# Attention and MLP block: three PV visits for four per group of MLP slots, and six PSUM banks shared by maxima and exps

## The chip, the cores and the metric

The kernel runs on one core of one Trainium2 chip. The metric is the device time of one execution in microseconds (us). Before the change the median of three runs is 1621.18 us.

## The reference

The input is layer-normalised; attention with 32 heads of 16 columns and an MLP (512 to 1792 to 512, squared ReLU) both read the normalised rows; the output is x plus attention times the SiLU of the MLP. All is fp32, 2048 rows.

```python
scores = jnp.einsum("bhqd,bhkd->bhqk", q, k) * (Dh ** -0.5)
p = _softmax(scores, axis=-1)
o = jnp.einsum("bhqk,bhkd->bhqd", p, v)
...
h = jnp.einsum("bsd,df->bsf", x, w1) + b1
r = jnp.where(h > zero, h, zero)
h = r * r
out = jnp.einsum("bsf,fd->bsd", h, w2) + b2
...
xn = _layernorm(x, axis=-1)
s = _A_ref(xn, A_wqkv, A_wo)
g = _silu(_B_ref(xn, B_w1, B_b1, B_w2, B_b2))
return x + s * g
```

## The kernel before

Work is cut into 32 units (four heads x 512 queries) of 16 key blocks (128 keys) each, so 512 slots. For every unit the kernel makes three things, each in its own stretch of time, one behind the other like a pipeline:

- the **maxima** ("m"): one matmul of queries against 512 keys into a PSUM bank (`max_mm`, matmul on L320), and VectorE's reduction of that bank to one column (L327). 64 per unit, four per slot, 24 slots ahead (LEAD). When a unit's last is made, `max_end` folds its maxima (L335), and six slots later `shift` transposes them (L371) and sends them through DRAM into rows of the unit's exp operands.
- the **exps** ("s"): one matmul of 128 keys against 512 queries of one head (`exp_mm`, L1286), whose operand rows already hold the subtracted maximum, and ScalarE's exp of that bank into SBUF (L1298). Four per slot.
- the **PV visit** (`pv_step`, `pv_mm`, L406): for one key block, four heads side by side in the four 32-column strips of the array, 512 queries each, added up in one bank (`po`) over 16 visits. Each of the four matmuls is two instructions in the trace (x8 per block). One visit stood at the end of every slot, for the block of two slots before.

Maxima and exps have a depth of 64 rows, so two of them run at once on the two row halves of the array; such a half is a "lane". Into the lane that is free goes the MLP: its matmuls are cut into 64-row halves too ("D"). A **round** is one instruction (or one pair of 256 columns) on each lane. Both lanes of a D accumulate into the same bank (`pd_t`), so the second lane may start only when the first is done with it: `block` gives the first D of a lane a wait (`last_use`) on the reader of a maximum or exp that the other lane issued after its last D.

Most MLP slots come in long groups of four (`block` yields 12 D units per lane, `long_slots` places them). First-layer groups (`first_pair`) have two 256-column matmuls per unit, second-layer groups (`second`) one of 512. A group before: ten rounds of lane 0's D with a maximum or exp on lane 1, a visit, two rounds with D and two with maximum and exp on both lanes, a visit; then the same with the lanes exchanged. That is 28 rounds, 16 maxima, 16 exps and four visits. When lane 1's D end, `post` has ScalarE read the bank `pd_t` (for the first layer two ReLUs, L568).

PSUM has eight banks: three in pool `pe` (`se`, for exps), three in pool `pm` (`pm_t`, for maxima), one `pd_t` and one `po`. A bank is used again, in turn within its pool, when its reader is done.

The order of TensorE, ScalarE, VectorE, GpSimd and the DMA queue (SP) is that in which the code issues (manual schedules); nothing is reordered. Slot ends also issue the loads and stores (`begin`, `max_end`, `shift_due`).

Of the kernel before, what the change touches and what calls it, by code (L numbers as in the profile page):

```python
# [9 lines left out]
F32 = mybir.dt.float32  # L10
# [7 lines left out]
P = 128  # L18
# [32 lines left out]
    [(0, 0), (0, 2), (1, 0), (1, 2), (2, 0), (2, 2)],  # L51
    [(0, 1), (0, 3), (1, 1), (1, 3), (2, 1), (2, 3)],
)
EPS = 1e-5


@with_exitstack
def kernel(
# [56 lines left out]
    with ExitStack() as ph:  # L115
# [136 lines left out]
        def block(mms, per, post, between={}):  # L252


            def emit(ms, lane, follow):
                r = slice(64 * lane, 64 * lane + 64)
                for out_, lh, rh, first_, last_ in ms:
                    mm = nc.tensor.matmul(  # L258
                        out_, lh(r), rh(r),
                        start=first_ and lane == 0, stop=last_ and lane == 1,  # L260
                        skip_group_check=True,
                    )
# [24 lines left out]

# [21 lines left out]
        for m4 in m4s:  # L309
            nc.vector.memset(m4, 0.0)  # L310

        def max_mm(j, bank=None):
            u, p, qb, kc = next(stream[j])
            qd = u // 4
# [5 lines left out]
            nc.tensor.matmul(  # L320
                ps,
                qms[u][p][64 * j : 64 * j + 64, qb * P : (qb + 1) * P],
                kas[qd, p][64 * j : 64 * j + 64, kc * 512 : (kc + 1) * 512],
                start=True, stop=True,
            )
            c = (2 * p + j) * 4 + qb
            return nc.vector.tensor_reduce(  # L327
                mxs[u][:, c, kc : kc + 1], ps, axis=AX.X, op=ALU.max
            )
# [948 lines left out]
        def exp_mm(st, j, pts, spare):  # L1278
            u, kb = divmod(st, 16)
            qd = u // 4  # L1280
            b = 64 * (j % 2)
            if spare:
                se = bank() if wos.get("banks") else pm.tile([P, 512], F32, name="pm_t")
            else:
                se = pe.tile([P, 512], F32, name="se")
            nc.tensor.matmul(  # L1286
                se, kas[qd, j // 2][b : b + 64, kb * P : (kb + 1) * P],
                qes[u][j // 2][b : b + 64, :],
                start=True, stop=True,
            )  # L1290
# [7 lines left out]
            return nc.scalar.activation(pts[j], se, AF.Exp, scale=0.25)  # L1298
# [201 lines left out]
        def dense():  # L1500
            mp = ExitStack()
            yield from mlp_tasks(mp)
            mp.close()
            early.close()
            wo_pools()
            wo_load(0, [0, 1, 2])
            wo_ask(0)
            wo_ask(1)
            for _ in range(2):
                yield [], None  # L1510
# [33 lines left out]
        def slot(st, mms, post):  # L1544
# [54 lines left out]
            for i in range(len(other)):  # L1599
                if i < len(own):  # L1600
                    own[i]()
                if spare and lane == 0 and i == len(mms) - 1:

                    use = nc.vector.tensor_scalar(seen, done_d[0][:, :1], 1.0, 0.0, op0=ALU.mult, op1=ALU.add)
                if other[i] is not None:
                    follow = other[i]()
                    if i >= len(own) - 1 and use is None:
                        use = follow
            last_use[0] = None if post is not None or spare and lane else use
            if post is not None:  # L1610
                post()
            max_end(g)

        def long_slots(st0, units, post):


            g0 = st0 + LEAD
# [4 lines left out]
            def s(lane):  # L1622
                kb, j = todo[lane].pop(0)
                return exp_mm(kb, j, pts[kb], False)

            for h in range(2):
                own, other = units[h], 1 - h
                for part, (mine, theirs) in enumerate((("D" * 10, "msmsmsmsms"), ("DDss", "mmsm"))):
                    st = st0 + 2 * h + part
                    if st > st0:  # L1630
                        begin(st)
                    for i, ops in enumerate(zip(mine, theirs)):
                        for lane in (h, other) if part else (other, h):
                            o = ops[0] if lane == h else ops[1]
                            if o == "D":
                                own.pop(0)()
                            elif o == "m":
                                max_mm(lane)
                            else:
                                use = s(lane)  # L1640
                                if part and lane == h and i == 2:
                                    last_use[0] = use
                        if part and h and i == 1 and post is not None:
                            post()
# [5 lines left out]
            assert not todo[0] and not todo[1] and not units[0] and not units[1]  # L1650

        def plain_slot(st):

# [14 lines left out]
        def begin(st):  # L1668
            now[0] = st
            if st % 64 == 48 and st // 64 + 1 < NQ:  # L1670
                load_v(st // 64 + 1)
            run_waiting()

        done = FIRST
        for st_ in range(NU * 16):
            if st_ < done:
                continue
            begin(st_)
            if st_ == FIRST:
                qs.close()  # L1680
            item = next(dn, None)
            if st_ == FIRST:

                for g in (LEAD, LEAD + 1):
                    max_end(g)
                for fn in last_store:
                    fn()
            if item is not None and len(item) > 2:
                assert st_ % 4 == 0
                long_slots(st_, *item[:2])  # L1690
# [9 lines left out]
            pv_step(st_ - 2, pts.pop(st_ - 2))  # L1700
        assert not [1 for it in stream for _ in it] and not left
        run_waiting(True)
        assert not waiting and next(dn, None) is None
# [29 lines left out]
```

## Time and profile before

| | |
|---|---|
| runs (three) | 1620.95 to 1621.23 us, median 1621.18 |
| profiled execution | span 1619.6 us from first to last instruction |
| granted TensorE clock | 1.00 throughout |
| stretch 165 to 1450 us (groups and other MLP slots) | TensorE busy 1285.0, VectorE 1132.1, ScalarE 992.7, GpSimd 380.4 us |
| idle time of VectorE ahead of maxima in that stretch | 151.8 us |

The profile comes from one execution. No time is shown for it but its span; the timed runs are 1.6 us longer than this. A busy share of TensorE says little, because matmuls overlap and their ends are modelled; start times of rounds and visits say more. In the rows, PE is the matmul, PEld the loading of its weights, which waits where a bank is not free. "64*128" and "128*32" name the rows and columns of the array that a matmul uses.

### The profile page before, as it was taken

To read this page: it belongs to the slowest core of one execution; us is meant where nothing else is said; L and a number is where in the kernel's file an instruction comes from. 1 tells how busy PE (TensorE), PEld (TensorE's weight loads), DVE (VectorE), ACT (ScalarE), POOL (GpSimd) and SP (SyncE) were. 2 spreads that over 40 slices of the span, in tenths; PEclk is the share of its full clock that TensorE was granted. 3 is DMA by queue.
4 is the path that set the end of the run, shared out by engine and by line. 5 is a ranking of instruction groups with operands and counts; after the bars stand their busy time and mean duration, and the time that the engine had idled before them with its cause. 6 is when DMAs were issued, how large, how long until landed. Compare 5 with 4: busy or idle time off the path is not lost.

```text
span 1619.6 us, 36065 instructions
## 1 busy us (share of the span) xinstructions
PE 1607.3 (99%) x13660; PEld 939.7 (58%) x13660; DVE 1352.4 (84%) x2307; ACT 1187.2 (73%) x2347; POOL 534.1 (33%) x610
## 2 busy tenths in 40 slices
PE   8999999999999999999999999999999999999998
PEld 7799665556545654664466446645654565445543
DVE  7486888888888888888888888888888888887754
ACT  7212777777777777877777777777777777778886
POOL 6436667133113311331133113311331123214621
PEclk9999999999999999999999999999999999999999
DMA  8967556434333333423333334323432252237655
GB/s 290 244 237 234 174 156 160 132 96 128 81 104 94 106 88 88 131 87 101 90 107 100 91 89 118 115 71 90 131 107 73 65 163 76 64 102 228 207 177 169
DMA packets 164173, 209.19 MB, mean 129 GB/s; under 512 B 59136, under 2 KB 79360, under 8 KB 162432
## 3 DMA queue, kind: packets, MB, share of 16 engines
q1 hardware_dynamic: 163856, 206.63, 43.9%
q8 instruction: 108, 1.77, 0.5%
q14 instruction: 65, 0.53, 0.1%
q10 hardware_dynamic: 144, 0.26, 0.0%
HBM read 148.90 MB, written 56.34 MB: 127 GB/s over the span
## 4 chain that ended last, share of the span: by engine, by line
PE 99%; DVE 1%; DMA 0%; issue 0%; ACT 0%; DVEq 0%
PE po L406 31%; PE pd_t L258 19%; PE pm_t L320 17%; PE se L1286 15%; PE pd_t L226 5%; PE pm_t L1157 4%; PE pm_t L226 1%; PE pd_t L1157 1%; PE se L1127 1%; PE se L1061 1%; PE se L320 1%; PE pm_t L1248 0%; PE pd_t L1127 0%; DVE mx L327 0%; PE po L1061 0%; DMA xt<-in_A_x_dram 0%
## 5 line engine op out<-in xcount | busy, mean ns | idle before, releaser
L327 DVE TENSOR_REDUCE mx<-pm_t 128x1 f32<-128x512 f32 x1910 | 1188.3, 684 | 174.5 <-PE pm_t L320 84.8
L1298 ACT ACTIVATE pt<-se 128x512 f32<-128x512 f32 x1894 | 975.4, 613 | 234.3 <-PE se L1286 187.0
L320 PE MATMUL pm_t<-ka,qm 64*128 64x512 f32 x1910 | 761.0, 419 | 0.0
L1286 PE MATMUL se<-qe,ka 64*128 64x512 f32 x2005 | 677.3, 396 | 0.0
L406 PE MATMUL po<-pt,v 128*32 128x512 f32 x3820 | 520.8, 605 | 0.2 <-DVE tsm L849 0.2
L320 PEld LDWEIGHTS pm_t<-ka,qm 64*128 64x128 f32 x1910 | 335.2, 184 | 236.0 <-DVE mx L327 224.5
L1286 PEld LDWEIGHTS se<-qe,ka 64*128 64x128 f32 x2005 | 338.9, 184 | 19.8 <-ACT xr L1298 1.7
L258 PEld LDWEIGHTS pd_t<-xc,w1s 64*128 64x128 f32 x2352 | 292.1, 187 | 82.2 <-issue 82.2
L258 PE MATMUL pd_t<-xc,w1s 64*128 64x256 f32 x2352 | 332.3, 288 | 0.0
L258 PE MATMUL pd_t<-w2t,hT 64*128 64x512 f32 x1080 | 300.1, 410 | 0.0
L258 PEld LDWEIGHTS pd_t<-w2t,hT 64*128 64x128 f32 x1080 | 179.3, 184 | 82.4 <-issue 75.5
L571 POOL TENSOR_TENSOR r<-r 128x512 f32<-128x512 f32 x56 | 58.2, 1040 | 353.5 <-ACT r L568 353.5
L406 PEld LDWEIGHTS po<-pt,v 128*32 128x32 f32 x3820 | 76.7, 108 | 147.1 <-issue 125.6
L327 DVE TENSOR_REDUCE mx<-se 128x1 f32<-128x512 f32 x121 | 77.9, 686 | 26.1 <-PE pm_t L1157 17.3
L590 POOL TENSOR_TENSOR u<-u,b_t 128x512 f32<-128x512 f32 x16 | 20.6, 1285 | 209.1 <-ACT u L589 209.1
L568 ACT ACTIVATE r<-pd_t,b_t 128x256 f32<-128x256 f32 x112 | 46.9, 470 | 57.1 <-PE pd_t L258 55.0
L99 POOL TENSOR_SCALAR sh<-tr 128x32 fp32r<-128x32 f32 x30 | 6.5, 217 | 213.6 <-DVE tr L371 213.6
L1157 PE MATMUL pm_t<-xT,wr_t 64*128 64x512 f32 x408 | 74.0, 388 | 0.0
L100 POOL TENSOR_TENSOR hT<-r,hT 128x512 fp32r<-128x512 f32 x56 | 72.2, 1290 | 4.7
L226 PE MATMUL pd_t<-w2t,hT 64*128 64x512 f32 x264 | 68.7, 392 | 0.0
L1157 PEld LDWEIGHTS pm_t<-xT,wr_t 64*128 64x128 f32 x408 | 60.7, 185 | 0.0
L455 POOL TENSOR_TENSOR ot<-ot,hl 128x512 f32<-128x512 f32 x27 | 34.7, 1285 | 65.4 <-DMA hl<-r_d 51.7
(177 smaller groups left out, 1398.9 us busy)
## 6 DMA issues: line engine op xcount, KB each, us to landing
w1s<-w_d SPq DMA_DIRECT2D x196, 256.0 KB
qm<-q_d SPq DMA_DIRECT2D x384, 32.0 KB
ka<-k_d SPq DMA_DIRECT2D x96, 128.0 KB
qe<-q_d SPq DMA_DIRECT2D x384, 32.0 KB
q_d<-hl SPq DMA_DIRECT2D x16, 512.0 KB
g<-g_d SPq DMA_DIRECT2D x32, 256.0 KB
k_d<-hl SPq DMA_DIRECT2D x15, 512.0 KB
on_d<-hl SPq DMA_DIRECT2D x116, 64.0 KB
```

Of the source, the lines that this page charges most:

```text
L100: (lo or nc.gpsimd).tensor_tensor(dst[1], raw, dst[0].bitcast(F32), op=ALU.subtract)
L226: mm = nc.tensor.matmul(out_, lh(r), rh(r), start=first_ and lane == 0, stop=last_ and lane == 1, skip_group_check=True,)
L258: mm = nc.tensor.matmul(out_, lh(r), rh(r), start=first_ and lane == 0, stop=last_ and lane == 1, skip_group_check=True,)
L320: nc.tensor.matmul(ps, qms[u][p][64 * j : 64 * j + 64, qb * P : (qb + 1) * P], kas[qd, p][64 * j : 64 * j + 64, kc * 512 : (kc + 1) * 512] ...
L327: return nc.vector.tensor_reduce(mxs[u][:, c, kc : kc + 1], ps, axis=AX.X, op=ALU.max)
L406: nc.tensor.matmul(po[32 * j : 32 * j + 32, :], vs[qd][:, (4 * kb + j) * VW : (4 * kb + j) * VW + 32], pts[j], start=(kb == 0), stop=(kb = ...
L455: nc.gpsimd.tensor_tensor(ot, ot, rb, op=ALU.mult)
L568: nc.scalar.activation(r[:, i], ps[:, i * CW : (i + 1) * CW], AF.Relu, bias=b1_t[:, fo : fo + 1])
L571: nc.gpsimd.tensor_tensor(r, r, r, op=ALU.mult)
L1157: mm = nc.tensor.matmul(out_, lh(r), rh(r), start=first_ and lane == first, stop=last_ and lane != first, skip_group_check=True,)
L1286: nc.tensor.matmul(se, kas[qd, j // 2][b : b + 64, kb * P : (kb + 1) * P], qes[u][j // 2][b : b + 64, :], start=True, stop=True,)
L1298: return nc.scalar.activation(pts[j], se, AF.Exp, scale=0.25)
```

## The change

`long_slots` gets its order from a string of 32 letters per group, m for a maximum and s for an exp, one for the first layer and one for the second. The group still has 28 rounds: 12 with lane 0's D, one with both lanes on maxima or exps, a visit of two key blocks, 12 with lane 1's D, a visit of one, three rounds with both lanes, a visit of one. The lane whose turn it is to start waits for the maximum or exp that the other lane issued in the round with both lanes. Slot ends fall behind rounds 7, 14, 21 and 28.

The six banks of `pe` and `pm` become one set (`spots`). A small account of times (`flow`, with constants for a round, a visit and the readers) is kept while the program is built; each maximum or exp takes the bank that this account expects to be free first. The account fixes which bank is used, and nothing else; at run time a matmul waits for its bank's real reader.

```diff
+DOUBLE = (12, 25, 26, 27)
+VISITS = {13: 2, 25: 1, 28: 1}
+QUARTERS = (7, 14, 21, 28)
+ORDERS = ("msmsmsmsmmsmmsmssmmsssmsmsmsssmm", "msmsmssmsmsmmsmssmmsmmssmssmssmm")
...
-            ], post, 4
+            ], post, ORDERS[per == 1]
...
+        def flow_start():
+            spots.extend([0, pe.tile([P, 512], F32, name="se")] for _ in range(3))
+            spots.extend([0, pm.tile([P, 512], F32, name="pm_t")] for _ in range(3))
+            flow["on"] = True
...
+        def flow_bank(kind):
+            at, t = spots.pop(min(range(len(spots)), key=lambda i: spots[i][0]))
+            flow["pe"] = max(flow["pe"], at)
+            every, held = READERS[kind]
+            begin_ = max(flow[kind], flow["pe"] + READY)
+            flow[kind] = begin_ + every
+            spots.append([begin_ + held, t])
+            return t
...
-            if spare:
+            if flow["on"]:
+                se = flow_bank("s")
+            elif spare:
...
-        def long_slots(st0, units, post):
+        def long_slots(st0, units, post, order):
...
+            ops, st, pv_at, fence = list(order), st0, st0 - 2, None
...
+            for r in range(len(order) - 4):
+                if r in QUARTERS:
+                    st += 1
+                    begin(st)
+                if r in DOUBLE:
+                    uses = [qk(lane) for lane in range(2)]
+                    done_lane = 0 if units[1] else 1
+                    if fence != done_lane:
+                        fence = done_lane
+                        last_use[0] = uses[done_lane]
+                else:
+                    h = 0 if units[0] else 1
+                    qk(1 - h)
+                    units[h].pop(0)()
+                    if not units[1] and post is not None:
+                        post()
+                flow_round()
+                if r + 1 in QUARTERS:
                     max_end(st + LEAD)
                     shift_due(st + 1 + LEAD)
-                    pv_step(st - 2, pts.pop(st - 2))
+                for _ in range(VISITS.get(r + 1, 0)):
+                    pv_step(pv_at, pts.pop(pv_at))
+                    pv_at += 1
+                if r + 1 in VISITS:
+                    flow_visit(VISITS[r + 1])
```

The order of TensorE in a first-layer group, first at the middle of the group. The rows are line, instruction, output and operands with buffer numbers, shape, and what the instruction waits for (DVE is VectorE, Activation ScalarE, DMAHW a load). Before, with D on L258, maxima on L320, exps on L1286 and PV on L406, from the tenth round on:

```order
L1286 MATMUL se_7326<-qe2_738,ka2_734 128x512 [waits Activation_49]
L258 MATMUL pd_t_7279<-xc_6197,w1s3_1510 128x256 x2
L406 MATMUL po_7240<-pt16_1494,v1_1789 32x512
L406 MATMUL po_7240<-pt10_1488,v1_1789 32x512
L406 MATMUL po_7240<-pt0_1478,v1_1789 32x512
L406 MATMUL po_7240<-pt12_1490,v1_1789 32x512
L258 MATMUL pd_t_7279<-xc_6197,w1s3_1510 128x256 x2
L320 MATMUL pm_t_7340<-ka0_207,qm0_204 128x512 [waits DVE_49]
L258 MATMUL pd_t_7279<-xc_6197,w1s3_1510 128x256 x2
L320 MATMUL pm_t_7345<-ka0_207,qm0_204 128x512 [waits DVE_49]
L1286 MATMUL se_7348<-qe2_738,ka2_734 128x512 [waits Activation_49]
```

Of the change (D on L268, maxima on L357, exps on L1325, PV on L443), the round with both lanes, the double visit and lane 1's first D:

```order
L357 MATMUL se_2470<-ka0_207,qm0_204 128x512 [waits DMAHW3_49,DMAHW4_49,DMAHW2_49,Activation_49]
L1325 MATMUL pm_t_2473<-qe3_739,ka3_735 128x512 [waits DVE_49]
L443 MATMUL po_6360<-pt1_1479,v1_1789 32x512
L443 MATMUL po_6360<-pt10_1488,v1_1789 32x512
L443 MATMUL po_6360<-pt0_1478,v1_1789 32x512
L443 MATMUL po_6360<-pt13_1491,v1_1789 32x512
L443 MATMUL po_6360<-pt2_1480,v1_1789 32x512
L443 MATMUL po_6360<-pt11_1489,v1_1789 32x512
L443 MATMUL po_6360<-pt3_1481,v1_1789 32x512
L443 MATMUL po_6360<-pt5_1483,v1_1789 32x512
L357 MATMUL pm_t_2472<-ka0_207,qm0_204 128x512 [waits Activation_49]
L268 MATMUL pd_t_6389<-xc_5531,w1s0_1507 128x256 [waits DVE_49]
```

The visit of one block that cut lane 0's D is gone and eight PV matmuls stand together; the exp ahead of them waits for VectorE, and so does lane 1's first D, for the maximum in the first row.

The second place is that of the banks, from round 6 of the same group on. Before:

```order
L320 MATMUL pm_t_7311<-ka0_207,qm0_204 128x512 [waits DVE_49]
L258 MATMUL pd_t_7279<-xc_6197,w1s2_1509 128x256 x2
L1286 MATMUL se_7316<-qe3_739,ka3_735 128x512 [waits Activation_49]
L258 MATMUL pd_t_7279<-xc_6197,w1s2_1509 128x256 x2
L320 MATMUL pm_t_7321<-ka0_207,qm0_204 128x512 [waits DVE_49]
L258 MATMUL pd_t_7279<-xc_6197,w1s2_1509 128x256 x2
```

Of the change:

```order
L357 MATMUL pm_t_2473<-ka0_207,qm0_204 128x512 [waits DVE_49]
L268 MATMUL pd_t_6389<-xc_5531,w1s2_1509 128x256 x2
L1325 MATMUL se_2470<-qe3_739,ka3_735 128x512 [waits Activation_49]
L268 MATMUL pd_t_6389<-xc_5531,w1s2_1509 128x256 x2
L357 MATMUL pm_t_2471<-ka0_207,qm0_204 128x512 [waits DVE_49]
L268 MATMUL pd_t_6389<-xc_5531,w1s2_1509 128x256 x2
L357 MATMUL se_2469<-ka0_207,qm0_204 128x512 [waits Activation_49]
L268 MATMUL pd_t_6389<-xc_5531,w1s3_1510 128x256 x2
L1325 MATMUL pm_t_2472<-qe2_738,ka2_734 128x512 [waits DVE_49]
```

Maxima now go into `se` banks and exps into `pm_t` banks, and either waits for the other's reader: the first row puts the group's fourth maximum into pm_t_2473, the bank that the exp of round 12 (second row of the piece above) takes next.

More of the change, by code (lines that the diff above doesn't have):

```diff
@@ L53 @@
 )
+DOUBLE = (12, 25, 26, 27)
+VISITS = {13: 2, 25: 1, 28: 1}
+QUARTERS = (7, 14, 21, 28)
+ORDERS = ("msmsmsmsmmsmmsmssmmsssmsmsmsssmm", "msmsmssmsmsmmsmssmmsmmssmssmssmm")
+ROUND = 232
+FIRST_ROUND = 335
+STEP = 907
+VISIT = 185
+READY = 450
+READERS = {"s": (476, 675), "m": (600, 745)}
 EPS = 1e-5
@@ L310, with flow_round, flow_visit @@
             nc.vector.memset(m4, 0.0)
+        flow = {"on": False, "pe": 0, "s": 0, "m": 0, "fresh": False}
+        spots = []
+        def flow_start():
+            spots.extend([0, pe.tile([P, 512], F32, name="se")] for _ in range(3))
+            spots.extend([0, pm.tile([P, 512], F32, name="pm_t")] for _ in range(3))
+            flow["on"] = True
+        def flow_round():
+            flow["pe"] += FIRST_ROUND if flow["fresh"] else ROUND
+            flow["fresh"] = False
+        def flow_visit(n):
+            flow["pe"] += VISIT + n * STEP
+            flow["fresh"] = True
+        def flow_bank(kind):
[6 more added lines that the diff above has]
+            return t
         def max_mm(j, bank=None):
             u, p, qb, kc = next(stream[j])
+            if bank is None and flow["on"]:
+                bank = lambda: flow_bank("m")
             qd = u // 4
@@ L1612, in slot @@
             max_end(g)
[L1614 to L1617 removed]
+        def long_slots(st0, units, post, order):
+            if not spots:
+                flow_start()
             todo = [[(st0 + k, j) for k in range(4) for j in (lane, lane + 2)] for lane in range(2)]
@@ L1620, in long_slots, with qk @@
                 pts.setdefault(kb, {})
-            def s(lane):
+            ops, st, pv_at, fence = list(order), st0, st0 - 2, None
+            def qk(lane):
+                if ops.pop(0) == "m":
+                    return max_mm(lane)
                 kb, j = todo[lane].pop(0)
                 return exp_mm(kb, j, pts[kb], False)
[L1626 to L1644, printed above, removed]
@@ L1645, in long_slots @@
                     max_end(st + LEAD)
                     shift_due(st + 1 + LEAD)
-                    pv_step(st - 2, pts.pop(st - 2))
+                for _ in range(VISITS.get(r + 1, 0)):
[3 more added lines that the diff above has]
+                    flow_visit(VISITS[r + 1])
             if post is not None:
                 last_use[0] = None
-            assert not todo[0] and not todo[1] and not units[0] and not units[1]
+            assert not ops and not todo[0] and not todo[1] and not units[0] and not units[1]
```

5 lines of the change are left out of this document (4 added, 1 removed).

## The prediction, made before the changed kernel ran

> **What bounds the kernel now.** I read the page first, then the chain of waits, then the timeline of single engines inside the MLP stretch.
>
> ```profile
> span 1619.6 us, 36065 instructions
> PE 1607.3 (99%) x13660; PEld 939.7 (58%) x13660; DVE 1352.4 (84%) x2307; ACT 1187.2 (73%) x2347; POOL 534.1 (33%) x610
> PE 99%; DVE 1%; DMA 0%; issue 0%; ACT 0%; DVEq 0%
> ```
>
> The third line is the chain that ended last: TensorE is 99% of it. VectorE is next with 84% busy. The chain in order of time shows the beat of the long groups: L406 x8 is one PV visit, and the second row of each pair is the fourth visit after the first (the three between are left out).
>
> ```profile
> 833.14 0.99 PE po L406 x8
> ...
> 844.55 1.00 PE po L406 x8
> ...
> 1058.79 1.00 PE po L406 x8
> ...
> 1070.12 0.99 PE po L406 x8
> ```
>
> So a group of four slots takes 844.55 - 833.14 = 11.41 us with 256-column MLP work (first layer) and 1070.12 - 1058.79 = 11.33 us with 512 columns (second layer). Their number comes from the MLP matmuls, grouped by form; a group issues 48 of the first kind or 24 of the second:
>
> ```profile
> L258 PE MATMUL pd_t<-xc,w1s 64*128 64x256 f32 x2352 | 332.3, 288 | 0.0
> L258 PE MATMUL pd_t<-w2t,hT 64*128 64x512 f32 x1080 | 300.1, 410 | 0.0
> L258 PE MATMUL pd_t<-ka,w1s 64*128 64x256 f32 x336 | 47.4, 287 | 0.0
> ```
>
> (2352 + 336) / 48 = 56 groups of the first kind, 1080 / 24 = 45 of the second, 101 in all. One microsecond more or less per ten groups is already 10 us. The timeline of TensorE gives the parts of a group; the columns are start, length, and instruction:
>
> ```profile
> 832.76 0.39 PE L1286 MATMUL se<-qe,ka 64*128 64x512 f32 x1
> 833.07 1.06 PE L406 MATMUL po<-pt,v 128*32 128x512 f32 x8
> 834.07 0.50 PE L258 MATMUL pd_t<-xc,w1s 64*128 64x256 f32 x2
> 834.41 0.40 PE L258 MATMUL pd_t<-xc,w1s 64*128 64x256 f32 x2
> 834.65 0.40 PE L258 MATMUL pd_t<-xc,w1s 64*128 64x256 f32 x2
> ...
> 836.33 0.40 PE L258 MATMUL pd_t<-xc,w1s 64*128 64x256 f32 x2
> 836.66 1.07 PE L406 MATMUL po<-pt,v 128*32 128x512 f32 x8
> ...
> 601.11 0.39 PE L258 MATMUL pd_t<-w2t,hT 64*128 64x512 f32 x1
> ...
> 602.98 0.39 PE L258 MATMUL pd_t<-w2t,hT 64*128 64x512 f32 x1
> ```
>
> From a round's start to the visit: 0.31 us (833.07 - 832.76) or 0.33 (836.66 - 836.33). From the visit to the next round: 1.00 (834.07 - 833.07). The first round behind a visit: 0.34 (834.41 - 834.07); any other: 0.24, and in the second layer 1.87 / 8 = 0.234.
>
> **What the change takes away.** The number of rounds stays 28. One visit of four goes and its key block moves into another visit. Only the end of the program shows several key blocks in one visit, three of them:
>
> ```profile
> 1605.41 0.62 PE L406 MATMUL po<-xl,v 128*32 128x512 f32 x1
> ...
> 1606.30 1.90 PE L406 MATMUL po<-xr,v 128*32 128x512 f32 x16
> 1608.13 0.50 PE L895 MATMUL pm_t<-wot,q 64*128 64x512 f32 x1
> ```
>
> Three blocks take 1608.13 - 1605.41 = 2.72, one takes 1.00, so each further one (2.72 - 1.00) / 2 = 0.86; the second alone reads 0.89 (1606.30 - 1605.41). I take 0.86. Per group that saves 1.00 - 0.86 on the block, 0.10 on a first round that becomes an ordinary one, and 0.08 on a last one: 0.32 us, 101 x 0.32 = 32 us at most. The Trainium skill (TensorEngine Tiling (Array Packing), Tiling Modes) says that changing the tiling mode drains the engine; the 1.00 against 0.86 agrees, and by that rule alone the result would be the first rival below, 1589.
>
> **What it adds: waits on VectorE.** The first phase now holds 13 rounds without a visit. In the first layer these issue maxima in rounds 0, 2, 4, 6, 8, 9, 11 and 12 (eight), in the second in 0, 2, 4, 7, 9, 11 and 12 (seven). VectorE's rows:
>
> ```profile
> 832.52 1.89 DVE L327 TENSOR_REDUCE mx<-pm_t 128x1 f32<-128x512 f32 x3 [0.54 <-PE pd_t L258]
> 834.60 3.08 DVE L327 TENSOR_REDUCE mx<-pm_t 128x1 f32<-128x512 f32 x5 [0.19 <-PE pd_t L258]
> 601.30 3.08 DVE L327 TENSOR_REDUCE mx<-pm_t 128x1 f32<-128x512 f32 x5 [0.19 <-PE pm_t L320]
> 602.64 0.18 PEld L320 LDWEIGHTS pm_t<-ka,qm 64*128 64x128 f32 x1 [0.19 <-DVE mx L327]
> 602.73 0.41 PE L320 MATMUL pm_t<-ka,qm 64*128 64x512 f32 x1
> ```
>
> A maximum lasts 0.68 (the first row of the next fence) and one follows the other every (3.08 - 0.68) / 4 = 0.60. The first starts 0.53 behind the round (834.60 - 834.07). A bank is free late: the second of the five from 601.30 ends at 601.30 + 0.60 + 0.68 = 602.58, the weight load that waited for it starts at 602.64, its matmul at 602.73, so 0.06 and 0.09 later.
>
> By the order on record the exp of round 12 goes into the bank of the fourth maximum (0, 2, 4, then 6 or 7). That one starts at 0.53 + 3 x 0.60 = 2.33, ends at 3.01, lets the load go at 3.07 and the matmul at 3.16. Without the wait round 12 starts at 0.34 + 11 x 0.24 = 2.98, or 2.91 in the second layer. So 0.18 or 0.25 us of TensorE time is lost ahead of the double visit, and behind the waiting exp stand the visit and every later round; nothing hides it. The double visit ends at 3.16 + 0.31 + 0.86 + 1.00 = 5.33.
>
> The first D of the other lane waits, in the first layer, for the eighth maximum: 0.53 + 7 x 0.60 + 0.68 + 0.06 = 5.47. Its load may come 0.34 - 0.24 = 0.10 behind the visit's end without loss, at 5.43; so 0.04 more. With seven maxima it is done at 4.87, free.
>
> The phases: A 5.37 (5.33 in the second layer); B, twelve rounds and a visit, 0.34 + 10 x 0.24 + 0.33 + 1.00 = 4.07 (4.01); C, three rounds and a visit, 0.34 + 0.24 + 0.31 + 1.00 = 1.89. Sums 11.33 and 11.23, against 11.41 and 11.33: 56 x 0.08 + 45 x 0.10 = **9.0 us saved** of the 32.
>
> **What else lands in the full phase.** Once per 16 slots VectorE also folds the maxima (L335) and transposes them (L371):
>
> ```profile
> 401.41 0.68 DVE L327 TENSOR_REDUCE mx<-pm_t 128x1 f32<-128x512 f32 x1
> 402.13 0.22 DVE L335 TENSOR_REDUCE m<-mx 128x16 f32<-128x64 f32 x1
> 402.29 1.89 DVE L327 TENSOR_REDUCE mx<-pm_t 128x1 f32<-128x512 f32 x3
> 416.69 0.20 DVE L371 STREAM_TRANSPOSE tr<-m 128x32 f32<-128x32 f32 x1
> ```
>
> The fold stretches 0.60 to 0.88 (402.29 - 401.41). It comes behind C's last maximum, where VectorE has 1.89 + 0.53 - (0.53 + 3 x 0.60) = 0.09 to spare, so 0.19 goes into phase A. The transpose now comes behind round 6, in phase A too: 0.20 less the overlap of 0.08, 0.12. Before, the idle 0.54 and 0.19 in the rows above took both. 28 units x 0.31 = 8.7 us at most, nothing at least; four or five of the transposes meet slots outside the groups, so I take 7.
>
> Edits at nothing: ScalarE,
>
> ```profile
> 832.79 0.84 ACT L568 ACTIVATE r<-pd_t,b_t 128x256 f32<-128x256 f32 x2 [1.03 <-PE pd_t L258]
> 833.52 4.01 ACT L1298 ACTIVATE pt<-se 128x512 f32<-128x512 f32 x8
> L1298 ACT ACTIVATE pt<-se 128x512 f32<-128x512 f32 x1799 | 923.8, 613 | 225.1 <-PE se L1286 180.3 <-PE pd_t L258 39.2 <-PE pm_t L320 4.4
> ```
>
> exps every (4.01 - 0.61) / 7 = 0.49, 16 per group and a pair of 0.84 make 8.7 of 11.3 us; the pair now has a visit, phase C and a visit (3.2 us) before the next group needs its bank, so it is covered; if two exps stood ahead of it, it would still be. PV of a block comes six rounds or more behind its last exp. What SP and POOL issue at slot ends moves by three rounds at most (slot ends at rounds 7, 14, 21, 28 in place of 10, 14, 24, 28), earlier everywhere; if a load were late after all, it would be q or k of the next unit, once per 16 slots. The 44 other MLP slots keep their orders and only get common banks: nothing, by the same 0.60 and 0.49.
>
> **Sum.** The span of 1619.6 lies 1.6 us under the median of 1621.2, which is taken as constant: 1621.2 - 9.0 + 7.0 = **1619 us**.
>
> The Trainium skill speaks against the change on the same page (Performance Considerations, PSUM Bottleneck): tiling speeds up TensorE and not the emptying of PSUM, which can become the bound. The rows agree with 0.60 us per maximum against 0.24 per round; without that page the sum is the same.
>
> **Rivals.** (1) The waits don't bite, because the maxima start earlier than the bank rows say: phase A is 2.98 + 0.31 + 1.86 = 5.15 or 5.08, everything is saved, 1621 - 32 = 1589. For it speaks that VectorE's mean share would be only 84% x 11.4 / 11.1; against it that 13 rounds last 3.3 us and their maxima 4.2 to 4.8. If half of each wait goes, 1604. (2) **Slower:** the second block of a visit costs nearly a whole visit in mid-program, because its operands come fresh from ScalarE there and not at the end: place, the 101 double visits; price up to 1.00 - 0.86 = 0.14 each, 14 us, 1633. It decides from 0.03 on, since only 2 us are left to lose. Then the change does not do what it says either. Against it is the row at 1606.30. (3) The late D restarts the pair. A late load elsewhere did:
>
> ```profile
> 915.20 0.40 PE L320 MATMUL pm_t<-ka,qm 64*128 64x512 f32 x1
> 915.47 0.18 PEld L1286 LDWEIGHTS se<-qe,ka 64*128 64x128 f32 x1 [0.29 <-ACT pt L1298]
> 915.82 0.39 PE L320 MATMUL pm_t<-ka,qm 64*128 64x512 f32 x1
> ```
>
> The round behind it came after 0.35 in place of 0.24. In 56 groups 0.11 is 6 us: 1625 to 1627 with the whole 8.7 above.
>
> **How the numbers follow.** Forecast (saved and lost nearly even, 1610 to 1625) 55%, of which 25 points lie under 1618, 27 within 0.2% and 3 above; rival 1, whole or half, 17%; rival 3, 16%, of which 2 within 0.2%; rival 2, 12%. A measurement of this kernel tells about 0.2%, 3.2 us, from no change. Faster 25 + 17 = 42%, same 27 + 2 = 29%, slower 3 + 14 + 12 = 29%. The range reaches up to rival 2's price, and down to past the half case of rival 1; its full case and the rest, under 2 in 10, stay out: 1599 to 1633.
>
> **What would show it.** In the changed profile: three visits per group, the double one 1.86 from start to next round (1.00 + 1.00 would be rival 2); a group of 11.33 and 11.23, not 11.1 (rival 1); TensorE's weight loads waiting for VectorE some 0.2 us once per group ahead of the double visit; groups with a fold or a transpose longer by 0.1 to 0.2. Wrong would be the whole if TensorE waited elsewhere, for ScalarE or a load, or if VectorE's interval changed with the common banks.

## The result, and the profile after

The changed kernel takes **1630.25 us** (median of four runs, 1630.05 to 1630.42), the kernel before beside it 1621.2 us. The ratio is 1.0055 with a 95% interval of 1.0043 to 1.0067: slower by about 0.55%. The forecast was 1619 us, so a little faster; the time lies inside the range of 1599 to 1633, on the wrong side of 1621.

The lines of the page that answer to those of before (span; busy time by engine; the chain that ended last):

```profile
span 1628.6 us, 37052 instructions
PE 1615.3 (99%) x13660; PEld 973.0 (60%) x13660; DVE 1348.9 (83%) x2307; ACT 1199.9 (74%) x2347; POOL 535.5 (33%) x610
PE 98%; ACT 1%; DVE 1%; issue 0%; DMA 0%; DVEq 0%
```

The span grew by 1628.6 - 1619.6 = 9.0 us, as the timed runs did. TensorE is still the chain. The page doesn't tell more, since TensorE counts as busy while rounds follow each other more slowly. The starts of the PV visits do (timeline of TensorE after the change; start, length, instruction; x8 is one key block, x16 two; L443 is L406 of before):

```profile
379.34 1.07 PE L443 MATMUL po<-pt,v 128*32 128x512 f32 x8
383.83 1.92 PE L443 MATMUL po<-pt,v 128*32 128x512 f32 x16
388.86 1.06 PE L443 MATMUL po<-pt,v 128*32 128x512 f32 x8
390.75 1.07 PE L443 MATMUL po<-pt,v 128*32 128x512 f32 x8
```

The phases, from here on always from visit to visit: A (a visit, 13 rounds) 383.83 - 379.34 = 4.49, B (the double visit, 12 rounds) 5.03, C (a visit, three paired rounds) 1.89. Read so for all groups, with the prediction's phases counted in the same way (A 1.00 + 3.16 + 0.31; B 1.86 + 0.04 + 3.07 in the first layer, 1.86 + 3.01 in the second):

| most frequent value, us | predicted, first / second layer | measured |
|---|---|---|
| A | 4.47 / 4.47 | 4.49 / 4.49 |
| B | 4.97 / 4.87 | 5.03 / 4.91 |
| C | 1.89 / 1.89 | 1.89 / 1.89 |
| group | 11.33 / 11.23 | 11.41 / 11.29 |
| group before, mean | | 11.405 / 11.324 |

Sums over the same stretch, from visits' starts too: the 56 first-layer groups take 643.7 us (638.7 before), the 45 of the second layer 512.2 (509.6), the 44 other MLP slots 129.3 (127.8). The differences, 5.0 + 2.6 + 1.5 = 9.1 us, are the whole loss of the span. Set against the forecast:

- **Plain groups** (the values of the table): 56 x (11.41 - 11.405) + 45 x (11.29 - 11.324) = -1.2, so 1.2 us saved, not 9.0.
- **Groups with something extra** in them: 643.7 + 512.2 - 56 x 11.41 - 45 x 11.29 = 8.9 us lost, not 7.0.
- **Other slots**: 1.5 lost, not nothing.

What made B slow is seen where the double visit ends (TensorE and VectorE after the change):

```profile
385.06 0.68 DVE L364 TENSOR_REDUCE mx<-se 128x1 f32<-128x512 f32 x1
385.68 0.50 PE L357 MATMUL se<-ka,qm 64*128 64x512 f32 x1
385.79 0.50 PE L268 MATMUL pd_t<-xc,w1s 64*128 64x256 f32 x2
...
388.43 0.39 PE L1325 MATMUL pm_t<-qe,ka 64*128 64x512 f32 x1
388.53 0.40 PE L268 MATMUL pd_t<-xc,w1s 64*128 64x256 f32 x2
388.86 0.64 PE L443 MATMUL po<-pt,v 128*32 128x512 f32 x4
```

The eighth maximum ends at 385.06 + 0.68 = 385.74, after lane 0 has begun (385.68). The first D on the other lane comes 0.11 behind it. Eleven rounds later its lane is still 0.10 behind (388.53 against 388.43), and the next visit comes 0.33 behind the late lane, as it does behind any single round. In 49 of the 56 first-layer groups the D comes 0.10 to 0.21 behind lane 0; in the other seven, which the next rows show, both start together and B is 4.92.

A second thing that the prediction had at nothing stands in the first group behind a second-layer chunk (visits, then ScalarE, then TensorE and its weight loads):

```profile
333.16 1.07 PE L443 MATMUL po<-pt,v 128*32 128x512 f32 x8
338.05 1.92 PE L443 MATMUL po<-pt,v 128*32 128x512 f32 x16
...
335.95 0.60 ACT L1337 ACTIVATE pt<-pm_t 128x512 f32<-128x512 f32 x1
336.43 0.64 ACT L632 ACTIVATE r<-u 128x512 f32<-128x512 f32 x1
336.95 1.10 ACT L1337 ACTIVATE pt<-se 128x512 f32<-128x512 f32 x2
...
337.61 0.18 PEld L357 LDWEIGHTS se<-ka,qm 64*128 64x128 f32 x1 [0.44 <-ACT pt L1337]
```

Phase A is 338.05 - 333.16 = 4.89 here, 0.4 above 4.49, and so it is in seven groups. The gate's tanh (L632) stands in ScalarE's queue between exps, and the last maximum's weight load waits for a bank that an exp still holds.

### The profile page after: what moved, and what is told of

Same layout as the page of the kernel before. It is cut to its first block, busy times and chain, and to the rows that moved or that the text cites. A ratio compares the mean times of both kernels' runs of the same rounds, so it can differ in the third digit from the quotient of the medians.

```text
span 1628.6 us, 37052 instructions
## 1 busy us (share of the span) xinstructions
PE 1615.3 (99%) x13660; PEld 973.0 (60%) x13660; DVE 1348.9 (83%) x2307; ACT 1199.9 (74%) x2347; POOL 535.5 (33%) x610
## 4 chain that ended last, share of the span: by engine, by line
PE 98%; ACT 1%; DVE 1%; issue 0%; DMA 0%; DVEq 0%
PE po L443 30%; PE pd_t L268 14%; PE se L357 11%; PE pm_t L357 10%; PE se L1325 9%; PE pm_t L1325 8%; PE pd_t L236 5%; PE pm_t L1194 4%; PE pm_t L236 2%; PE pd_t L1194 1%; PE se L1164 1%; PE se L1098 1%; ACT pt L1337 1%; PE pm_t L1285 0%; PE pd_t L1164 0%; DVE mx L364 0%
## 5 line engine op out<-in xcount | busy, mean ns | idle before, releaser
L364 DVE TENSOR_REDUCE mx<-se 128x1 f32<-128x512 f32 x1012 | 662.9, 683 | 118.3 <-PE se L357 52.6
L364 DVE TENSOR_REDUCE mx<-pm_t 128x1 f32<-128x512 f32 x1019 | 662.2, 682 | 95.1 <-PE pm_t L357 62.9
L1337 ACT ACTIVATE pt<-se 128x512 f32<-128x512 f32 x1007 | 569.7, 609 | 131.6 <-PE se L1325 63.2
L1337 ACT ACTIVATE pt<-pm_t 128x512 f32<-128x512 f32 x903 | 514.3, 609 | 131.8 <-PE pm_t L1325 62.8
L443 PE MATMUL po<-pt,v 128*32 128x512 f32 x3820 | 499.9, 602 | 0.2 <-DVE tsm L886 0.2
L1325 PE MATMUL se<-qe,ka 64*128 64x512 f32 x1118 | 432.1, 414 | 0.0
L357 PE MATMUL se<-ka,qm 64*128 64x512 f32 x1012 | 400.1, 417 | 1.3 <-ACT pt L1337 1.0
L357 PE MATMUL pm_t<-ka,qm 64*128 64x512 f32 x1019 | 399.1, 415 | 0.1
L1325 PE MATMUL pm_t<-qe,ka 64*128 64x512 f32 x929 | 360.7, 417 | 0.0
L268 PE MATMUL pd_t<-xc,w1s 64*128 64x256 f32 x2352 | 313.2, 286 | 0.0
L268 PEld LDWEIGHTS pd_t<-xc,w1s 64*128 64x128 f32 x2352 | 290.1, 186 | 0.2
L268 PE MATMUL pd_t<-w2t,hT 64*128 64x512 f32 x1080 | 287.1, 410 | 0.0
L357 PEld LDWEIGHTS se<-ka,qm 64*128 64x128 f32 x1012 | 181.6, 184 | 156.8 <-ACT pt L1337 99.5
L357 PEld LDWEIGHTS pm_t<-ka,qm 64*128 64x128 f32 x1019 | 181.0, 184 | 137.6 <-ACT pt L1337 92.2
L1325 PEld LDWEIGHTS se<-qe,ka 64*128 64x128 f32 x1118 | 197.6, 184 | 46.9 <-ACT pt L1337 24.4
L443 PEld LDWEIGHTS po<-pt,v 128*32 128x32 f32 x3820 | 87.1, 108 | 169.6 <-issue 156.4
L1325 PEld LDWEIGHTS pm_t<-qe,ka 64*128 64x128 f32 x929 | 163.4, 184 | 41.5 <-ACT pt L1337 23.5
L268 PEld LDWEIGHTS pd_t<-w2t,hT 64*128 64x128 f32 x1080 | 181.0, 184 | 4.4
```

Of the source, the lines that this page charges most:

```text
L268: mm = nc.tensor.matmul(out_, lh(r), rh(r), start=first_ and lane == 0, stop=last_ and lane == 1, skip_group_check=True,)
L357: nc.tensor.matmul(ps, qms[u][p][64 * j : 64 * j + 64, qb * P : (qb + 1) * P], kas[qd, p][64 * j : 64 * j + 64, kc * 512 : (kc + 1) * 512] ...
L364: return nc.vector.tensor_reduce(mxs[u][:, c, kc : kc + 1], ps, axis=AX.X, op=ALU.max)
L443: nc.tensor.matmul(po[32 * j : 32 * j + 32, :], vs[qd][:, (4 * kb + j) * VW : (4 * kb + j) * VW + 32], pts[j], start=(kb == 0), stop=(kb = ...
L1325: nc.tensor.matmul(se, kas[qd, j // 2][b : b + 64, kb * P : (kb + 1) * P], qes[u][j // 2][b : b + 64, :], start=True, stop=True,)
```

## The experiments

Each ratio is to the kernel before, run beside it on the same chip.

**1. The first D waits for an exp and not for the maximum.** (Round numbers count from 0, as in `DOUBLE`; "behind round 13", as in `VISITS`, means behind the thirteenth.) In the paired round 12 the code makes lane 1's first D wait for the reader of lane 0's instruction, the eighth maximum. Here it waits for the reader of the exp beside it:

```diff
-                        last_use[0] = uses[done_lane]
+                        last_use[0] = uses[1]
```

> The changed kernel, except that the first D of lane 1 waits for the exp that is issued beside the eighth maximum in round 12, and no longer for that maximum. Theory (the wait for the eighth maximum brings the D load some 0.11 us late in the first layer, every time, and this shifts its whole lane): phase B of the 56 groups falls from 5.03 to 4.92 us, with a transpose by 0.2 at most; 56 x 0.10 plus about 12 x 0.09 are 6 to 7 us, so 1623 to 1625 us. Rival (VectorE's load as such sets the pace, through the banks, and whoever waits last is the same): phase B stays at 5.03, 1629 to 1631 us.

Measured: 1625.3 us, ratio 1.0025 (1.0014 to 1.0035). B in the first layer is 4.92 or 4.93; its sum over 56 groups falls from 281.6 to 276.0 us. Such a place, in its timeline of TensorE:

```profile
371.63 1.92 PE L443 MATMUL po<-pt,v 128*32 128x512 f32 x16
373.49 0.49 PE L357 MATMUL se<-ka,qm 64*128 64x512 f32 x1
373.49 0.50 PE L268 MATMUL pd_t<-xc,w1s 64*128 64x256 f32 x2
...
376.55 1.07 PE L443 MATMUL po<-pt,v 128*32 128x512 f32 x8
```

Both lanes start together, as in all 56 groups, and 376.55 - 371.63 = 4.92. The late D is shown, at 5 us. It isn't the whole loss: 4 us stay above before. The exp is on lane 1 itself; what makes it a witness for lane 0 is that it is issued behind lane 0's last D. At this place the second half of that D starts at 371.07, the exp's reader ends at 372.40 and the eighth maximum's at 373.63.

**2 and 3. Half of VectorE's work, in the changed kernel and in the one before.** The softmax only needs some shift, so the maximum over half of the columns will do here. The edit in the changed kernel; the other kernel has the same one:

```diff
-                mxs[u][:, c, kc : kc + 1], ps, axis=AX.X, op=ALU.max
+                mxs[u][:, c, kc : kc + 1], ps[:, :256], axis=AX.X, op=ALU.max
```

> The changed kernel, with each maximum taken over the first 256 of its 512 columns; the other half of the maxima is left out. VectorE then needs about half as long per maximum, 0.33 in place of 0.60 us from one to the next. Theory (the 0.32 us per group that the visits save are there, and waits for VectorE take them back): 1621 - 32 = 1589 us if nothing else waits, up to 1600 us if ScalarE's exps then wait in part. Rival (the second block of a visit or the order of the rounds itself is dear): 1615 to 1630 us.

> The kernel before, with the same halved maxima. Theory (in the kernel before nothing in the groups waits for VectorE beyond some tenths of a microsecond): 1612 to 1621 us, so most of what the halved maxima bring to the changed kernel is not brought here. Rival (VectorE is the bound of both kernels in the same measure): about 1590 us, as far below as the changed kernel with halved maxima.

Measured: 1604.76 us (0.9898, 0.9882 to 0.9913) for the changed kernel, 1615.85 (0.9965, 0.9952 to 0.9979) for the one before. So a faster VectorE is worth 25.5 us to the changed kernel and 5.4 to the old one: most of the loss is VectorE's, as the first theory says. But 1604.76 is above its upper end of 1600, and 11 us under its partner, not 32. A VectorE at 56% busy doesn't let the merged visits pay in full either. The phases say where (visits with halved maxima):

```profile
373.19 1.06 PE L443 MATMUL po<-pt,v 128*32 128x512 f32 x8
377.55 1.92 PE L443 MATMUL po<-pt,v 128*32 128x512 f32 x16
382.47 1.06 PE L443 MATMUL po<-pt,v 128*32 128x512 f32 x8
...
376.46 1.23 ACT L1337 ACTIVATE pt<-se 128x512 f32<-128x512 f32 x2
377.12 0.18 PEld L357 LDWEIGHTS se<-ka,qm 64*128 64x128 f32 x1
```

B is 4.92, but A is 377.55 - 373.19 = 4.36 in both layers. Thirteen rounds without any wait would be 1.00 + 0.34 + 11 x 0.24 + 0.31 = 4.29, and 4.22 with the 0.234 of the second layer. What holds up the last round there is ScalarE: the load of the last maximum starts at 377.12, 0.05 behind the end (377.07) of the first of the two exps in the row above it. The seven first groups behind a second-layer chunk stay at 4.88, so those are not VectorE's. Waits in A (56 x 0.07 + 45 x 0.14 = 10 us) and these seven groups (7 x 0.52 = 3.6 us) are most of the 21 us that are missing.

**4. The double visit elsewhere.** Eight maxima in a row of 13 rounds looked like too many, so here all four paired rounds come last and the visits are spread out:

```diff
-DOUBLE = (12, 25, 26, 27)
-VISITS = {13: 2, 25: 1, 28: 1}
+DOUBLE = (24, 25, 26, 27)
+VISITS = {12: 2, 20: 1, 28: 1}
...
-ORDERS = ("msmsmsmsmmsmmsmssmmsssmsmsmsssmm", "msmsmssmsmsmmsmssmmsmmssmssmssmm")
+ORDERS = ("msmsmsmmsmmsmsmssmsmmsmsmssmmsss", "msmsmsmmsmmsmsmssmsmmsmsmssmmsss")
...
```

The order of maxima and exps changes with it, and so does what lane 1's first D waits for.

> The changed kernel with the three visits in another place: the double visit behind round 11, ahead of the last paired exp of lane 0's D, single ones behind rounds 19 and 27; seven maxima and not eight ahead of the double visit, and the first D of lane 1 waits for an exp issued right behind lane 0's last D, not for a maximum. Theory (the loss is made of the two waits for VectorE around the double visit; spread evenly, the same visits save nearly all): a group takes 11.1 to 11.2 us in place of 11.50 and 11.38, so 1593 to 1605 us. Rival (VectorE needs 16 x 0.60 us and its extras per group, and the wait turns up in another place): 1618 to 1630 us.

Measured: 1728.19 us (1.0662, 1.0647 to 1.0677). Neither expectation. Visits, then ScalarE:

```profile
373.48 1.93 PE L443 MATMUL po<-pt,v 128*32 128x512 f32 x16
377.44 1.06 PE L443 MATMUL po<-pt,v 128*32 128x512 f32 x8
382.05 1.07 PE L443 MATMUL po<-pt,v 128*32 128x512 f32 x8
...
379.75 0.59 ACT L1337 ACTIVATE pt<-se 128x512 f32<-128x512 f32 x1
380.23 0.84 ACT L605 ACTIVATE r<-pd_t,b_t 128x256 f32<-128x256 f32 x2
380.94 0.62 ACT L1337 ACTIVATE pt<-se 128x512 f32<-128x512 f32 x1
```

The phase behind the double visit is free of waits (8 rounds, 3.96 = 1.86 + 0.34 + 6 x 0.24 + 0.32). The last one takes 4.61, where 1.00 + 0.34 + 6 x 0.24 + 0.32 = 3.10 would do: it issues twelve maxima and exps in eight rounds, and the two ReLUs stand ahead of five exps with no visit to cover them. In the changed kernel a visit follows the last D at once. The forecast's sentence that the visits cover that pair held there. Without them the phase loses 1.5 us per first-layer group; about 0.8 of it needs no ReLUs, since the second layer, which has none there, mostly takes 3.90 in the same eight rounds. The ReLUs' share is then some 0.7.

**5. The tanh one slot later**, on top of experiment 1:

```diff
-                    later(2, gate)
+                    later(3, gate)
```

> The kernel of the first experiment (first D of lane 1 waits for an exp) with the gate's tanh queued one slot later, so behind the double visit and not in the rounds ahead of it. Theory (the tanh, 0.64 us in ScalarE's queue, is not covered in phase A: seven first groups take 4.88 in place of 4.49 us there, some fourteen second-layer groups 4.59): phase A is 4.5 in all of these, 7 x 0.39 + 14 x 0.09 = 4 us less than 1625, so 1621 to 1622.5 us. Rival (it costs the same wherever it lands, or these 4.88 come from the w1 and x loads of a new chunk): 1624.5 to 1626 us.

Measured: 1622.57 us (1.0008, 0.9999 to 1.0017), no longer told apart from the kernel before, and 2.7 us less than experiment 1, which is 7 x 0.39. No first-layer phase A is above 4.7 any more. The 4.59 of the second layer stayed, so that part of the theory fell: it isn't the tanh. In their stretches stands a transpose (L408), which experiment 8 takes up.

**6. Own banks in the 44 other slots**, on top of experiment 1:

```diff
         def slot(st, mms, post):
+            flow["on"] = False
...
-            if not spots:
+            if not flow["on"]:
+                spots.clear()
                 flow_start()
```

> The kernel of the first experiment, with the six common banks only in the groups of four, and the three and three banks of before in the 44 other MLP slots. Theory (the common banks make a slot 2.94 in place of 2.90 us, 1.5 us in all): 1623 to 1624.5 us. Rival (the 0.04 per slot come from the groups around them, which end and begin with another order): no change, 1625 us.

Measured: 1624.25 us (1.0020, 1.0011 to 1.0029), inside the interval of experiment 1. The time lies in the theory's range, but not for the theory's reason. More than half of the slots went from 2.94 to 2.88, but six take 3.2 where two did, and the sum stayed (129.8 against 129.9 us). What makes the slots 1.5 us longer than before is open; the banks alone it isn't.

**7. The merging alone undone**, on top of experiment 1:

```diff
-VISITS = {13: 2, 25: 1, 28: 1}
+VISITS = {6: 1, 13: 1, 25: 1, 28: 1}
```

> The kernel of the first experiment with the double visit taken apart again: one visit behind round 6, one behind round 13; orders and banks stay. This undoes the merging alone. Theory (the merging is worth 0.32 us per group to TensorE, and the 13 rounds in a row lose about 0.2 of it to waits for VectorE): phase A's waits go, a group is 11.38 to 11.4 us in place of 11.31, so 5 to 10 us more, 1630 to 1635 us. Rival (the merging as such brings nothing, it is all given back by the waits): 1625 us or less.

Measured: 1636.07 us (1.0093, 1.0079 to 1.0107), 10.8 us more than experiment 1 and 1 us above the theory's range. So the change can be taken in three steps: the order and the common banks, without the merging and without the late D, lose 1636.1 - 1621.2 = 14.9 us; merging two visits gains 10.8; the late D loses 5.0: 14.9 - 10.8 + 5.0 = 9.1. No run has the new order with the banks of before, or the old order with common banks, so how the 14.9 us split between order and banks isn't shown. The visits here:

```profile
366.46 1.06 PE L443 MATMUL po<-pt,v 128*32 128x512 f32 x8
368.35 1.07 PE L443 MATMUL po<-pt,v 128*32 128x512 f32 x8
370.97 1.07 PE L443 MATMUL po<-pt,v 128*32 128x512 f32 x8
373.82 1.06 PE L443 MATMUL po<-pt,v 128*32 128x512 f32 x8
377.95 1.06 PE L443 MATMUL po<-pt,v 128*32 128x512 f32 x8
```

Six rounds take 2.62 and seven 2.85, both free of waits (1.00 + 0.34 + 4 or 5 x 0.24 + 0.31 = 2.61 or 2.85); twelve take 4.13 in place of 4.05. In the second layer the seven take 2.94, 0.1 more than without waits, and the twelve 4.12, also 0.1 more. So a plain group takes 11.48 and 11.54, not the 11.38 to 11.4 that were expected, and most of the 14.9 us are the second layer's: its groups sum to 518.7 us (509.6 before), the first layer's to 643.0 (638.7), the other slots to 129.4 (127.8).

**8. Fold and transpose ahead of the double visit**, on top of experiments 5 and 6. `fold` is the first half of `max_end`, taken out; in the groups it and the transpose of the first quarter run behind round 13:

```diff
                 if r + 1 in QUARTERS:
-                    max_end(st + LEAD)
-                    shift_due(st + 1 + LEAD)
+                    max_end(st + LEAD, False)
+                    if r + 1 != 7:
+                        shift_due(st + 1 + LEAD)
+                if r + 1 == 13:
+                    fold(st + LEAD - 2)
+                    shift_due(st + 1 + LEAD)
```

> The kernel of the experiment with the late tanh, with own banks in the 44 slots, and with the fold of the maxima and the transpose that hit phase A queued right ahead of the double visit, where VectorE stood idle 0.5 us or more. Theory (the fold costs phase A 0.17 us in some 22 groups and the transpose 0.09 in 14, only because they land in the phase in which banks wait for VectorE): phase A is 4.49 in all groups, 22 x 0.17 + 14 x 0.09 = 5 us less than 1622.6, and up to 1 for the banks: 1616.5 to 1618.5 us, just under the kernel before. Rival (the same work delays the next maxima wherever it stands): 1621 to 1623 us.

Measured: **1617.29 us (0.9976, 0.9967 to 0.9985)**, the only version with whole maxima that is faster than the kernel before, by 0.24%. VectorE in the changed kernel, and behind the dots in this one:

```profile
403.01 0.68 DVE L364 TENSOR_REDUCE mx<-pm_t 128x1 f32<-128x512 f32 x1
403.72 0.22 DVE L372 TENSOR_REDUCE m<-mx 128x16 f32<-128x64 f32 x1
403.86 1.28 DVE L364 TENSOR_REDUCE mx<-pm_t 128x1 f32<-128x512 f32 x2
...
404.54 0.68 DVE L364 TENSOR_REDUCE mx<-se 128x1 f32<-128x512 f32 x1
405.14 0.21 DVE L372 TENSOR_REDUCE m<-mx 128x16 f32<-128x64 f32 x1
405.70 0.69 DVE L364 TENSOR_REDUCE mx<-se 128x1 f32<-128x512 f32 x1 [0.35 <-PE pd_t L268]
```

The fold stood between two maxima of phase A; now VectorE has 0.35 us to spare behind it. A is 4.49 or 4.50 in all 56 first-layer groups, and the 4.58 of the second layer are gone but for two: 2.7 and 2.8 us less in the two layers' sums.

**9. The double visit ahead of the 13 rounds and not behind them**, on top of experiments 5 and 6:

```diff
-VISITS = {13: 2, 25: 1, 28: 1}
+VISITS = {13: 1, 25: 1, 28: 2}
```

> The kernel of the experiment with the late tanh, with own banks in the 44 slots and the double visit at the group's end: one visit behind round 13, one behind round 25, two behind round 28. The 13 rounds now follow the double visit, in which the banks run empty; fold and transposes stay at the group's end. Theory (how much a run of rounds loses is set by how many of the six banks are still full when it begins): phase A behind the double visit is at most 5.25 from visit to visit, in place of 4.49 + 0.86 = 5.35, phase B behind a single one 4.12, as with four visits; in all some 0.05 us per group less, and the folds fall into the double visit: 1611 to 1618 us. Rival (the loss is set by the number of rounds in a row alone): 1621 to 1626 us.

Measured: 1635.17 us (1.0086, 1.0073 to 1.0100). The theory fell:

```profile
366.81 1.92 PE L443 MATMUL po<-pt,v 128*32 128x512 f32 x16
372.16 1.06 PE L443 MATMUL po<-pt,v 128*32 128x512 f32 x8
376.55 1.07 PE L443 MATMUL po<-pt,v 128*32 128x512 f32 x8
```

Phase A behind the double visit is 372.16 - 366.81 = 5.35: 4.49 and a second block's 0.86. The longer pause beforehand brings A nothing. It does bring B something in the first layer: behind a single visit B is mostly 4.19, and 4.38 in eleven groups, where behind the double one it took 4.92 - 0.86 = 4.06. That, and twelve C phases of 2.36 to 2.50, put the total above the rival's, too.

**10. The paired round of phase A as its first**, on top of experiment 8:

```diff
-DOUBLE = (12, 25, 26, 27)
+DOUBLE = (0, 25, 26, 27)
...
-ORDERS = ("msmsmsmsmmsmmsmssmmsssmsmsmsssmm", "msmsmssmsmsmmsmssmmsmmssmssmssmm")
+ORDERS = ("msssmmsmsmmmmsssmsmsssmsmmssmmms", "msssmmsmsmmmmsssmsmsssmsmmssmmms")
...
```

> The kernel of the experiment with the moved fold and transpose, with the paired round of phase A as its first and not its last: rounds 0, 25, 26 and 27 are paired, both layers have one order with eight maxima in phase A, and the first D of lane 1 waits for the exp issued right behind lane 0's last D. The 13 rounds in a row still issue 14 matmuls into the six banks. Theory (what counts is how fast matmuls are issued where no bank has come back yet; the first round lasts 0.34 us anyway, so a second matmul there is nearly free, and the last round, now a single one, doesn't start late): phase A 4.40 to 4.45 in place of 4.49 us, 1608 to 1614 us. Rival (14 matmuls in 13 rounds wait the same wherever the paired round stands): 1616 to 1619 us.

Measured: 1640.51 us (1.0122, 1.0106 to 1.0139), worse than both. Two visits around phase A:

```profile
367.72 1.06 PE L447 MATMUL po<-pt,v 128*32 128x512 f32 x8
372.38 1.92 PE L447 MATMUL po<-pt,v 128*32 128x512 f32 x16
```

4.66 in place of 4.49. The order moved too, with four maxima behind each other near the end of the phase, and ScalarE now holds rounds up inside it (in this phase the weight load at 371.46 waits 0.19 us for an exp). So this run doesn't tell the place of the paired round from the order.

## Why the prediction was wrong

**The step that failed** is the one on the first D of the other lane: "Its load may come 0.34 - 0.24 = 0.10 behind the visit's end without loss, at 5.43; so 0.04 more." When the wait ends was nearly right: the load was put at 0.14 behind the visit's end (5.47 against 5.33), and the D came 0.11 behind it. That 0.10 of this are free was wrong. A late load isn't taken in by the slow first round: the lane keeps its delay for twelve rounds and hands it to the next visit (385.68 and 385.79, then 388.43 and 388.53). Phase B took 5.03 where 4.97 was forecast, 56 x 0.06 = 3.4 us, and experiment 1, which takes the whole delay away, gains 5.0 us. With this term alone put right the forecast would have been 1619 + 3.4 = 1622.4, already slower than 1621.2. Rival 3, for which 16% were given, named the place and nearly the price (6 us). Its mechanism was that the whole next round comes later; the rows show one late lane beside one that is hardly held up.

It is the largest of several misses that add up to 11 us. The rest are terms too small or put at nothing:

- **"Edits at nothing: ScalarE"**: seven times 0.39, 2.7 us (experiment 5). The sentence costed the ReLUs, which are covered, and didn't ask what else ScalarE does now and then: the tanh runs 16 times, and seven of these fall into phase A of a first-layer group. Before, seven of them fell into first-layer stretches of four rounds, which took 2.12 us like the others.
- **"The 44 other MLP slots ... nothing"**: 1.5 us, cause open.
- **Waits in A and B**: 0.02 too little in A (101 x 0.02 = 2.0 us), 0.04 in B of the second layer (1.8 us, cause open).
- **The beat before**, read from one group as 11.41 and 11.33, is 11.405 and 11.324 in the mean: 0.6 us.

On the other side, fold and transpose cost 0.8 us less than the 7.0 forecast.

What was right, first of all, is the wait for VectorE ahead of the double visit, and its mechanism. TensorE, its weight loads, VectorE and ScalarE in the changed kernel:

```profile
380.33 0.49 PE L357 MATMUL pm_t<-ka,qm 64*128 64x512 f32 x1
...
382.60 0.61 ACT L1337 ACTIVATE pt<-se 128x512 f32<-128x512 f32 x1
382.67 1.28 DVE L364 TENSOR_REDUCE mx<-pm_t 128x1 f32<-128x512 f32 x2
382.81 0.49 PE L1325 MATMUL se<-qe,ka 64*128 64x512 f32 x1
383.14 0.39 PE L357 MATMUL pm_t<-ka,qm 64*128 64x512 f32 x1
383.27 0.19 PEld L357 LDWEIGHTS se<-ka,qm 64*128 64x128 f32 x1
383.40 0.18 PEld L1325 LDWEIGHTS pm_t<-qe,ka 64*128 64x128 f32 x1
383.40 0.50 PE L1325 MATMUL pm_t<-qe,ka 64*128 64x512 f32 x1
383.83 0.64 PE L443 MATMUL po<-pt,v 128*32 128x512 f32 x4
```

The phase's first round starts at 380.33. Its fourth maximum, the first of the two in VectorE's row, ends at 382.67 + 0.68 = 383.35, and the load of round 12's exp starts at 383.40, 3.07 behind the first round, as worked out. It is 3.07 in all 59 phases A that take 4.49 or 4.50. From there to the visit are 0.42 or 0.43, where 0.09 + 0.31 were counted: that is the 0.02 that A lacked. Rounds ahead of it wait too (0.33 and 0.26 in place of 0.24; the load at 383.27 for the exp that ends at 383.21), but the last wait covers them. With halved maxima ScalarE holds up the last round instead (experiment 2). Right were also:

- The second block costs 0.86: 385.68 - 383.83 = 1.85 from visit to round, against 1.00. Rival 2 falls.
- C, and the value of A: 4.47 predicted, 4.49 measured. VectorE's waits take back most of what the visits save, so rival 1 falls; experiments 2 and 3 agree. The Trainium skill (TensorEngine Tiling (Array Packing), Performance Considerations) says that emptying PSUM can become the bound once tiling has made TensorE faster; 25.5 us from halved maxima after the change against 5.4 before agree.
- Fold and transpose: 7.0 us predicted; the 8.9 of all extras without the tanh's 2.7 are 6.2, and moving them brought 5.5 in phase A (experiment 8).

So the forecast had 32 us to gain and 30 to lose. Each part was sized to within a few us, and the difference was smaller than the errors of its parts. The merging by itself does gain (10.8 us, with tanh and fold where they were); the order and the common banks that came with it lose 14.9, and the late D 5.0 (experiments 1 and 7).

**What a stretch loses, by its length**, from the plain phases (the single visit ahead of each is counted in):

| rounds / maxima and exps in a row | kernel | measured | without waits |
|---|---|---|---|
| 3 / 6 | changed | 1.89 | 1.00 + 0.34 + 0.24 + 0.31 = 1.89 |
| 7 / 8 | experiment 7 | 2.85 | 2.85 |
| 7 / 8, second layer | experiment 7 | 2.94 | 1.00 + 0.34 + 5 x 0.234 + 0.31 = 2.82 |
| 10 / 10 | before | 3.58 | 1.00 + 0.34 + 8 x 0.24 + 0.31 = 3.57 |
| 12 / 12, second layer | experiment 7 | 4.12 | 1.00 + 0.34 + 10 x 0.234 + 0.31 = 3.99 |
| 13 / 14, second layer | changed | 4.49 | 4.22 |

In the first layer six banks carry about ten matmuls in a row at 0.24 each when a reader needs 0.5 to 0.6 for each and starts half a microsecond late. With fourteen, 0.2 to 0.27 us are lost, nearly the 0.32 that the merging brings. The number alone doesn't set it: in the second layer eight already lose 0.12, experiment 10 lost more with the same fourteen, and halved maxima lost less (4.36). The rows also differ in order and in how the banks are shared, so which of these sets the loss isn't shown.

## What to carry to other kernels

Where work is merged to save a fixed cost, ask what the old breaks were good for: here each visit let two readers catch up with six banks, and a longer stretch without one exposed every small thing in their queues. A wait should hang on the earliest witness there is: the exp issued beside the maximum, whose reader ended 1.2 us earlier, gave 5 us. A sum of two large terms that nearly cancel should get a range, and chances, as wide as the errors of its terms.

## What the runs showed of the hardware

- **A late row half stays late.** Of two lanes on the two row halves, the one that starts 0.11 us late is still 0.10 late eleven rounds on, without catching up and hardly slowing the other, whose twelfth round starts 2.75 behind its first and 2.72 without the delay (experiment 1). The next visit waits for both. No delay here was longer than 0.21.
- **A last round that had to wait also holds up the visit behind it.** The visit comes 0.43 after it (383.83 behind 383.40), in place of 0.31 to 0.33; it is 0.42 or 0.43 in all 101 phases A. The row of the matmul that waited reads 0.50 and not 0.39.
